# Two chosen experts per query instead of all four: attention on rows of x, VectorE transposes, 32-row value tiles

## The chip, the cores and the metric

The kernel runs on one core of a Trainium2 chip. The metric is the device time of one execution in microseconds (us). The core has five engines that each work through their own list of instructions: PE (TensorE, matmul and weight loads), DVE (VectorE), ACT (ScalarE), POOL (GpSimd) and SP, which issues most DMAs. They meet only at semaphores.

## The reference

There are four batches of S = 1088 positions. Two blocks follow each other.

1. A sketched attention without softmax. For each of four heads of 32 numbers, `phi(x)` is the outer product of two 8-number sketches, `S1 x` and `S2 x`, so 64 features. With `kv = phi(k)^T v` and `z = sum phi(k)`, the result is `phi(q) kv / (phi(q) z + 1e-6)`. The heads side by side give x, 1088 x 128 per batch.
2. A mixture of four attention experts on x:

```
logits = x @ w_gate ; topk = the two largest of the four, per position
w = softmax over the two chosen logits
for each expert e:
    q, k, v = x @ wq[e], x @ wk[e], x @ wv[e]          # 128 -> 64
    a = softmax(causal(q k^T / 8))                     # 1088 x 1088
    out += (w of e, where e was chosen) * (a @ v @ wo[e])
```

All numbers are float32. The reference computes every expert for every query and then masks; a query's two other experts do not reach the result.

## The kernel before, in words

Queries and keys come in tiles of 128 (nine of them, the last with 64 rows). For each batch, `prepare` (line 210) makes what the experts need. `sketch` (253) multiplies k and q by the sketches and forms the features, `kvs` (290) sums them, `turn_features` (305) transposes q's features, and `numer` (316) makes numerator and denominator and divides into `xs`. `turn_x` (338) transposes x to `xT`. Then `project` (354) makes q and k of two experts at a time, 512 columns each, `project_v` (365) makes the values of all four experts and the gate's logits, and `gate` (371) ranks the logits.

The attention goes in units of two query tiles and one pair of experts (`units`, 562). For each query tile and expert of the pair, `scores` (441) runs a matmul with 64 rows (q of the expert times k of the expert, line 452). `take` (432) adds the mask and finds the row's maximum on DVE while it copies the scores from PSUM to SBUF. `soften` (437) takes the exponential on ACT. `turns_of` (504) transposes the weights with TensorE, 128 x 128 at a time through PSUM (512), and `evacuate` (66) copies them back, twice on ACT and once on DVE in turn (69, 71). `values` (578) multiplies with the expert's values, 64 output rows per expert (584, 627). `gates` (529) turns the gate weight over the softmax sum (542), line 589 multiplies it in, and `output` (641) applies wo (658) and stores.

All four experts are computed for all queries; the gate's weight is zero where an expert was not chosen.

The order on PE is written out by hand (line 666 on): for each unit the scores come first, then the values of an earlier unit, then the transposes of the unit before, with the pieces of the next batch's preparation woven in between (`weave`, 550). The order on the other engines is left to a scheduler. PSUM is a pool of eight banks of 512 columns, each handed out as it comes free (`bank`, 73), so scores of several tiles can wait in PSUM at once.

Of the kernel before, what the change touches and what calls it, by code (L numbers as in the profile page):

```python
# [19 lines left out]
def kernel(  # L20
# [15 lines left out]

# [11 lines left out]

    cp = ctx.enter_context(tc.tile_pool(name="const", bufs=1))
    p2 = ctx.enter_context(tc.tile_pool(name="p2", bufs=2))
    p4 = ctx.enter_context(tc.tile_pool(name="p4", bufs=4))
    ps = ctx.enter_context(tc.tile_pool(name="ps", bufs=8, space=bass.MemoryType.PSUM))
# [6 lines left out]

    turn = [0]

    def evacuate(out_, in_):
        turn[0] += 1
        if turn[0] % 3 == 0:
            nc.vector.tensor_copy(out_, in_)  # L69
        else:  # L70
            nc.scalar.copy(out_, in_)  # L71

    def bank(name):
        return ps.tile([128, 512], F32, tag="bank", name=name)
# [9 lines left out]
    kvz = const("kvz", [128, 2, D + 1])  # L84

    def load_rows(dst, src, b):
        return nc.sync.dma_start(out=dst, in_=src[b].rearrange("h (t c) d -> (h t) (c d)", c=C))
# [12 lines left out]
    def load(b):  # L100
        load_rows(kin, k, b)
        load_rows(qin, q, b)
        load_v(b)


# [4 lines left out]
    idle = const("idle", [128, 128])  # L110
    nc.vector.memset(idle, 0.0)
    for x, s in enumerate((S1, S2)):
        eng = (nc.sync, nc.scalar)[x]
        if NS == 1:
            ins = eng.dma_start(out=raw[R * x : R * x + R], in_=s)
        else:
            ins = eng.dma_start(out=raw[R * x : R * x + R].rearrange("p d w -> p (d w)"), in_=s.bitcast(I32))
        if x == 0:
            landing = ins
            with tc.issue_after(landing.ins):  # L120
                load(0)
    wqk = const("wqk", [128, 2, E, HD])
    wvg = const("wvg", [128, E * HD + E])
    wo_sb = const("wo", [128, NG, DM])
    with tc.issue_after(landing.ins):
        for x, w in enumerate((wq, wk)):
            nc.sync.dma_start(out=wqk[:, x], in_=w.rearrange("e p d -> p e d"))
        nc.sync.dma_start(
            out=wvg[:, 0 : E * HD].rearrange("p (e d) -> p e d", e=E), in_=wv.rearrange("e p d -> p e d"))
        nc.sync.dma_start(out=wvg[:, E * HD :], in_=w_gate)  # L130
        nc.sync.dma_start(out=wo_sb, in_=wo.rearrange("(g e) h d -> (e h) g d", g=NG))
    if NS == 2:

# [3 lines left out]
        ex, sg, ma, lw = (const(f"S_{n}", [32, 32], I32) for n in ("ex", "sg", "ma", "lw"))  # L137
        lead, last, ok = (const(f"S_{n}", [32, 32]) for n in ("lead", "last", "ok"))
# [33 lines left out]
    SKW = const("SKW", [128, NS, 2, 2, R])  # L172
    nc.gpsimd.memset(SKW, 0.0)

    nc.vector.transpose(ST.rearrange("p n d -> p (n d)"), S_sum.rearrange("p n d -> p (n d)"))
    for h in range(H):
        last = (nc.vector.tensor_copy, nc.scalar.copy, nc.gpsimd.tensor_copy, nc.vector.tensor_copy)[h](
            SKW[32 * h : 32 * h + 32, :, :, h % 2, :], ST[:, :, 0 : 2 * R].rearrange("d n (x r) -> d n x r", x=2))
    mark = [last.ins]

    nc.gpsimd.memset(kT[:, S:], 0.0)
    nc.gpsimd.memset(qT[:, S:], 0.0)
    nc.gpsimd.memset(vp[:, :, :, D:], 1.0)
    nc.gpsimd.memset(vp[64:, NJ - 1, :, 0:D], 0.0)

# [3 lines left out]


# [11 lines left out]
    vts = [const(f"vt{n}", [128, NJ, E * HD + E]) for n in range(2)]  # L202
    for t in vts:
        nc.gpsimd.memset(t[64:, NJ - 1, E * HD :], 0.0)


    nc.scalar.mul(wqk[:, 0], wqk[:, 0], scale)


    def prepare(b):  # L210
        first = b == 0
        xT = p2.tile([128, S], F32, tag="xT", name=f"xT{b}", bufs=1)
        qk = p2.tile([128, 2 * NG, S], F32, tag="qk", name=f"qkT{b}")
        vt = vts[b % 2]
# [38 lines left out]
        def sketch(nm, xT_, j0, j1):  # L253
# [31 lines left out]
            if first:  # L285
                mark[0] = ins.ins
# [454 lines left out]
```

## Time and profile before

| | us |
|---|---|
| median of 3 runs (lowest, highest) | 372.27 (372.18, 372.96) |
| span of the profiled execution | 362.4 |
| median less span | 9.9 |
| PE busy | 351.5 (97%) |
| weight loads (PEld) busy | 252.2 (70%) |
| DVE busy | 238.7 (66%) |
| ACT busy | 227.7 (63%) |
| POOL busy | 54.1 (15%) |
| share of the chain that ended last: PE | 87% |

The record holds no separate time of the profiled execution beside its span; what lies around the span is read as the difference to the median. Rows of the profile are grouped by source line, engine, operation and tiles: "sc<-qkT" is a matmul that writes the tile sc from qkT. A group shows its busy time, the mean of one instruction in nanoseconds, the idle time of the engine ahead of it, and what ended that. PEld is the load of a matmul's stationary operand, which can overlap a running matmul. The granted PE clock was full (1.000) over the whole span.

### The profile page before, as it was taken

Reading aid. Unit: us, or ns where it says so; the run is one execution under the profiler, and the core shown is the slowest. Engines: PE = TensorE matmul, PEld = TensorE weight load, DVE = VectorE, ACT = ScalarE, POOL = GpSimd, SP = SyncE. Lnnn points to the kernel's source line nnn. Section 1 sums busy time; section 2 is a strip of 40 time slices with the busy share of each in tenths; the row PEclk is TensorE's granted clock in tenths of the full one; section 3 lists DMA queues with packets and bytes.
Section 4 is the critical chain, followed back from the end, with each engine's and each line's share of the span. In section 5 each row is a group of like instructions: output and inputs, shape, how many; then the busy total and the mean of one; then the engine's idle time right before and its main releaser. Section 6 shows DMA issues by size and latency. Waiting matters only on the chain.

```text
span 362.4 us, 10207 instructions
## 1 busy us (share of the span) xinstructions
PE 351.5 (97%) x4138; PEld 252.2 (70%) x4138; DVE 238.7 (66%) x808; ACT 227.7 (63%) x557; POOL 54.1 (15%) x77
## 2 busy tenths in 40 slices
PE   8799989999999999999999999999999999999995
PEld 4666659678676777787675857876776656677774
DVE  6559996676656866657846766567755756765652
ACT  2436757658646786666665756856585666746782
POOL 4001184000000552000000281000000010000010
PEclk9999999999999999999999999999999999999999
DMA  7152422100000000000000000000000000000001
GB/s 208 39 173 59 144 74 96 34 3 16 2 14 1 20 5 2 14 4 4 14 16 0 4 19 4 15 2 2 16 16 2 2 14 6 1 2 16 14 5 29
DMA packets 11374, 10.09 MB, mean 28 GB/s; under 512 B 3648, under 2 KB 10304, under 8 KB 11328
## 3 DMA queue, kind: packets, MB, share of 16 engines
q1 hardware_dynamic: 11168, 9.38, 9.4%
q8 instruction: 32, 0.52, 0.6%
q14 instruction: 14, 0.11, 0.1%
q10 hardware_dynamic: 160, 0.07, 0.1%
HBM read 7.22 MB, written 2.23 MB: 26 GB/s over the span
## 4 chain that ended last, share of the span: by engine, by line
PE 87%; DVE 7%; ACT 3%; issue 1%; DMA 0%; DVEq 0%; ACTq 0%
PE tp L512 18%; PE av L584 17%; PE sc L452 15%; PE qk L356 7%; PE po L658 4%; PE vg L368 4%; PE av L542 3%; PE av L627 3%; PE kv L298 2%; PE num L324 2%; PE sc L493 2%; PE tq L310 2%; ACT a L439 2%; PE sc L470 2%; DVE a L434 1%
## 5 line engine op out<-in xcount | busy, mean ns | idle before, releaser
L439 ACT ACTIVATE a<-a,mx 128x256 f32<-128x256 f32 (+8 forms) x136 | 107.5, 792 | 68.9 <-DVE mx L434 68.9
L434 DVE CUSTOM_DVE_ANT_0 a<-sc,mask 128x512 f32<-128x512 f32 (+3 forms) x136 | 74.2, 592 | 22.5 <-PE sc L452 16.8
L512 PE MATMUL tp<-ident,a 128*128 128x128 f32 (+1 forms) x648 | 85.4, 273 | 0.3 <-ACT aT L71 0.3
L512 PEld LDWEIGHTS tp<-ident,a 128*128 128x128 f32 (+1 forms) x648 | 74.2, 140 | 14.7 <-issue 7.7
L71 ACT COPY aT<-tp 128x512 f32<-128x512 f32 (+3 forms) x121 | 62.5, 547 | 12.6 <-PE tp L512 11.3
L584 PE MATMUL av<-aT,vt 128*64 128x256 f32 (+1 forms) x640 | 67.5, 362 | 0.0
L584 PEld LDWEIGHTS av<-aT,vt 128*64 128x64 f32 x640 | 43.3, 137 | 29.9 <-DVE mx L434 8.1
L452 PE MATMUL sc<-qkT 64*128 64x512 f32 (+3 forms) x320 | 63.4, 531 | 0.0
L536 POOL TENSOR_TENSOR rb<-gw,r 128x256 f32<-128x256 f32 (+1 forms) x36 | 21.1, 590 | 258.1 <-DVE r L533 151.2
L69 DVE COPY aT<-tp 128x512 f32<-128x512 f32 (+3 forms) x59 | 36.9, 628 | 18.9 <-PE tp L512 18.7
L452 PEld LDWEIGHTS sc<-qkT 64*128 64x128 f32 x320 | 27.7, 186 | 25.2 <-issue 15.1
L532 DVE TENSOR_SCALAR r<-z 128x4 f32<-128x4 f32 (+1 forms) x36 | 7.5, 207 | 48.4 <-ACT a L439 46.7
L434 DVE CUSTOM_DVE_ANT_0 a<-sc,mask,mx 128x512 f32<-128x512 f32 (+3 forms) x72 | 38.2, 567 | 0.0
L356 PE MATMUL qk<-xT,wqk 128*128 128x512 f32 x64 | 31.4, 601 | 0.5 <-ACT xT L71 0.5
L439 ACT ACTIVATION_READ_ACCUMULATOR a<-a,mx 128x1 f32 x136 | 25.5, 187 | 0.0
L368 PE MATMUL vg<-wvg,xT 128*128 128x260 f32 (+1 forms) x72 | 20.6, 389 | 0.3 <-ACT xT L71 0.3
L71 ACT COPY qkT<-qk 128x512 f32<-128x512 f32 x20 | 11.7, 583 | 11.8 <-PE qk L356 11.8
L658 PE MATMUL po<-wo,yT 128*128 128x128 f32 (+1 forms) x136 | 18.7, 277 | 0.1
L434 DVE DVE_READ_ACCUMULATOR2_ANT mx<- 128x1 f32 x216 | 17.7, 82 | 0.0
L658 PEld LDWEIGHTS po<-wo,yT 128*128 128x128 f32 (+1 forms) x136 | 16.5, 187 | 0.9 <-issue 0.5
L544 ACT COPY rs<-av 128x256 f32<-128x256 f32 (+1 forms) x36 | 11.9, 352 | 8.3 <-PE av L542 8.0
L589 DVE TENSOR_TENSOR yT<-av,rs 128x256 f32<-128x256 f32 x32 | 12.5, 409 | 5.9 <-ACT rs L544 5.9
(123 smaller groups left out, 355.6 us busy)
## 6 DMA issues: line engine op xcount, KB each, us to landing
kin<-in_k_dram SPq DMA_DIRECT2D x4, 544.0 KB, 3.7
qin<-in_q_dram SPq DMA_DIRECT2D x4, 544.0 KB, 5.9
vin<-in_v_dram SPq DMA_DIRECT2D x16, 128.0 KB, 4.9
out_dram<-ob SPq DMA_DIRECT2D x15, 128.0 KB, 1.8
vtl<-in_v_dram SPq DMA_DIRECT2D x8, 16.0 KB, 2.2
wqk<-in_moe_wq_dram SPq DMA_DIRECT2D x1, 128.0 KB, 5.1
wqk<-in_moe_wk_dram SPq DMA_DIRECT2D x1, 128.0 KB, 3.6
wvg<-in_moe_wv_dram SPq DMA_DIRECT2D x1, 128.0 KB, 4.2
```

Source lines behind the costliest of these rows:

```text
L69: nc.vector.tensor_copy(out_, in_)
L71: nc.scalar.copy(out_, in_)
L356: nc.tensor.matmul(t, wt(a), xT[:, 512 * c : 512 * c + 512], start=True, stop=True)
L368: nc.tensor.matmul(t[0:m, 0 : E * HD + E], xT[:, 128 * j : 128 * j + m], wvg, start=True, stop=True)
L434: nc.vector.tensor_tensor_reduce(out=dst, in0=src, in1=msk, scale=-1.0, scalar=most, op0=ALU.add, op1=ALU.min, accum_out=mx)
L439: nc.scalar.activation(out=a, in_=a, func=ACTF.Exp, bias=mx, scale=-1.0, accum_out=z)
L452: nc.tensor.matmul(sc[e], qk[rows, g, 128 * i : 128 * i + 128], qk[rows, NG + g, keys], start=True, stop=True)
L512: nc.tensor.transpose(tp[0:nk, x : x + 128], ats[e][:, 128 * j : 128 * j + nk], ident)
L536: nc.gpsimd.tensor_tensor(out=rb[:, 0 : w // 128].rearrange("p x (e d) -> p x e d", d=HD), in0=gws[:, :, :, None].to_broadcast(wide), in1= ...
L584: nc.tensor.matmul(av[HD * e : HD * e + HD, lo:256], vt[:, j, c : c + HD], aT[:, e, j, lo:256], start=(j == 0), stop=(j == 2 * p + 1))
L589: nc.vector.tensor_tensor(out=yT[:, g], in0=av[:, 0:256], in1=rs, op=ALU.mult)
L658: nc.tensor.matmul(po[0:nq, DM * x : DM * x + DM], yT[:, g, 128 * x : 128 * x + nq], wo_sb[:, g], start=(g == 0), stop=(g == NG - 1))
```

## The change

Each query now has two rows instead of four: one for each expert that the gate chose. The scores are written with x itself as keys. For an expert, q k^T is x (wq wk^T) x^T, so `expert_matrices` makes the four 128 x 128 products `mcat` once. `chosen` multiplies a tile of x with all four (one matmul of 512 columns), and picks two of the four results per query: ACT copies experts 0 and 3 into the two slots of `u`, and four `copy_predicated` on DVE write experts 1 and 2 over them where `sel` says so. `turn_chosen` transposes `u` to `uT`. A score row is then `uT` times `xT`, 128 deep.

The values are x too: the weights are multiplied with x, and the product goes through wv of the slot's three possible experts (`heads`), where the gate's weight is zero for all but the chosen one. `put` applies wo.

The weights are no longer transposed by TensorE. DVE transposes them in blocks of 32 x 32 (`turns` in `step`, `last_step`), which leaves key k of a block on partition k of one of four groups of 32 partitions, and the query group r = 0 to 3 decides the partition group. So `values` runs matmuls of 32 rows in four partition groups, r = 0 to 3, each into its own PSUM bank (4 to 7), and x must stand four times, once in each partition group: `spread_x` copies it with 16 DMAs per batch.

PSUM is now one tile of eight banks. Scores use banks 0 to 3, always two rows of up to 1024 columns; all other work turns over banks 4 to 7, one bank or an even pair (`bank`). Transposes on TensorE (`turn_blocks`) go in halves of 64 rows.

The order is written out on PE, DVE and ACT. Each batch has six steps, with the query tiles (4, 2), (5, 1), (3), (6, 0), (7) and (8). A step gives the scores, takes and exponentials of its tiles, then the DVE transposes of the step before (`left`), then the work listed in `gaps_of`: values of groups A (tiles 0, 6, 7, 8; done in the next batch's first step), B (4, 5) and C (1, 2, 3), the outputs, and the next batch's preparation. Sketches always run in two accumulated parts; the feature products of later batches stay on POOL. At the start, DVE's transposes of k and half of q now come ahead of the splitting of S1 and S2 into float32 parts.

The diff, cut to its core:

```diff
-    ps = ctx.enter_context(tc.tile_pool(name="ps", bufs=8, space=bass.MemoryType.PSUM))
+    ps = ctx.enter_context(tc.tile_pool(name="ps", bufs=1, space=bass.MemoryType.PSUM))
...
+    P = ps.tile([128, 8, 512], F32, tag="P", name="P")
+    flat = P.rearrange("p k c -> p (k c)")
+    def bank(n=1):
+        k = turn[0] % 4
+        if n == 2 and k % 2:
+            k = (k + 1) % 4
+        turn[0] = k + n
+        return 4 + k
...
+    xrep = const("xrep", [128, NC, DM])
+    GROUPS = {"B": (4, 5), "C": (1, 2, 3), "A": (0, 6, 7, 8)}
+    COL = {"B": 0, "C": 128, "A": 0}
...
+    def spread_x(b):
+        for s in range(4):
+            nj = (NC - s + 3) // 4
+            for r in range(4):
+                nc.sync.dma_start(out=xrep[32 * r : 32 * r + 32, s : s + 4 * (nj - 1) + 1 : 4],
+                                  in_=xs[32 * s : 32 * s + 32, 0:nj])
+    def turn_blocks(ins, dst, copy=None):
+        n, k0 = len(ins), bank(2)
+        for x, a in enumerate(ins):
+            for h in range(2):
+                rows = slice(64 * h, 64 * h + 64)
+                nc.tensor.transpose(P[:, k0 + h, 64 * x : 64 * x + 64], a[rows], ident[rows, rows])
+        (copy or nc.scalar.copy)(dst.rearrange("p n (h q) -> p n h q", h=2),
+                                 P[:, k0 : k0 + 2, 0 : 64 * n].rearrange("p h (n q) -> p n h q", n=n))
...
+    def expert_matrices():
+        wT = p2.tile([128, 2, NG, DM], F32, tag="a", name="wT", bufs=3)
+        for x in range(2):
+            turn_blocks([wqk[:, x, 2 * g : 2 * g + 2, :].rearrange("p e d -> p (e d)") for g in range(NG)], wT[:, x])
+        k0 = bank(2)
+        for g in range(NG):
+            for e in range(2):
+                rows = slice(64 * e, 64 * e + 64)
+                nc.tensor.matmul(P[:, k0 + e, DM * g : DM * g + DM], wT[rows, 0, g], wT[rows, 1, g],
+                                 start=True, stop=True)
+        nc.scalar.mul(mcat.rearrange("p (g e) d -> p e g d", g=NG),
+                      P[:, k0 : k0 + 2, 0 : NG * DM].rearrange("p e (g d) -> p e g d", g=NG), scale)
...
-        def project(a, c):
...
-        def project_v(j):
...
+            nc.tensor.matmul(P[:, k0, E * j : E * j + E], m_.xT[:, 128 * j : 128 * j + 128], wg, start=True, stop=True)
+        V.tensor_tensor(out=pr, in0=ch[:, :, 0::2], in1=ch[:, :, 1::2], op=ALU.mult)
+        V.tensor_copy(sel[:, :, 0:4:3], ch[:, :, 0:4:3])
+        V.tensor_copy(sel[:, :, 2:5:2], pr[:, :, ::-1])
+        V.tensor_tensor(out=sel[:, :, 1:6:4], in0=ch[:, :, 1:3], in1=pr, op=ALU.subtract)
...
+    def chosen(b, i):
+        m_, k0 = batch(b), bank()
+        nc.tensor.matmul(P[:, k0], m_.xT[:, 128 * i : 128 * i + 128], mcat.rearrange("p e d -> p (e d)"),
+                         start=True, stop=True)
+        u = p4.tile([128, 2, DM], F32, tag="u", name=f"u{b}_{i}", bufs=3)
+        c = P[:, k0].rearrange("p (e d) -> p e d", e=E)
...
+        nc.scalar.copy(u[:, 0], c[:, 0])
+        nc.scalar.copy(u[:, 1], c[:, 3])
+        V = nc.vector
+        for x in (1, 2):
+            for s in range(2):
+                V.copy_predicated(u[:, s], m_.sel[:, i, 3 * s + x : 3 * s + x + 1].bitcast(I32).to_broadcast([128, DM]),
+                                  c[:, x])
+        return u
...
-    def scores(b, i, g, qk, z):
...
-    def turns_of(name, i, ats, aT, q0):
...
-    def gates(name, z, gws, w):
...
+    def step(b, tiles):
+        m_, name = batch(b), f"{b}_{tiles[0]}"
+        a = p2.tile([128, 2, 1024], F32, tag="a", name=f"a{name}", bufs=3)
+        mx = p4.tile([128, 2, 2], F32, tag="mx", name=f"mx{name}")
+        at, base = {}, 0
+        for i in tiles:
+            at[i] = base
+            base += 128 * i + 128
+        for s in range(2):
+            for i in tiles:
+                c, end = at[i], at[i] + 128 * i + 128
+                while c < end:
+                    n = min(end, c // 512 * 512 + 512) - c
+                    nc.tensor.matmul(flat[:, 1024 * s + c : 1024 * s + c + n], m_.uT[:, i, s],
+                                     m_.xT[:, c - at[i] : c - at[i] + n], start=True, stop=True)
+                    c += n
+        for s in range(2):
+            for x, i in enumerate(tiles):
+                n = 128 * i + 128
+                cols = slice(at[i], at[i] + n)
+                m = mx[:, s, x : x + 1]
+                take(a[:, s, cols], flat[:, 1024 * s + at[i] : 1024 * s + at[i] + n], mask[:, 1024 - n :], m)
+                soften(a[:, s, cols], m, m_.z[:, i, s : s + 1])
+        def turns():
+            for i in tiles:
+                n, u0 = blocks(i), unit(i)
+                nc.vector.transpose(aT[GRP[i]][:, 0:n, u0 : u0 + 2].rearrange("p c s k -> p s c k"),
+                                    a[:, :, at[i] : at[i] + 32 * n].rearrange("p s (c k) -> p s c k", k=32))
+        return turns
...
+    def last_step(b):
...
+    def values(b, grp):
+        tiles, units = GROUPS[grp], UNITS[grp]
+        last = {(i, r): min(4 * i + r, NC - 1) for i in tiles for r in range(4)}
+        for c in range(blocks(tiles[-1])):
+            for r in range(4):
+                us = [x for x, (i, s) in enumerate(units) if c <= last[i, r]]
+                if us:
+                    assert us[-1] == len(units) - 1
+                    rows = slice(32 * r, 32 * r + 32)
+                    nc.tensor.matmul(P[:, 4 + r, COL[grp] + 32 * us[0] : COL[grp] + 32 * len(units)],
+                                     xrep[rows, c], aT[grp][rows, c, us[0] :],
+                                     start=(c == 0), stop=(c == max(last[i, r] for i in tiles)), skip_group_check=True)
+    def keep(b, c0, k0, n):
+        nc.scalar.copy(batch(b).yT[:, k0 : k0 + n].rearrange("p u r q -> p r u q"),
+                       P[:, 4:8, c0 : c0 + 32 * n].rearrange("p r (u q) -> p r u q", q=32))
...
+    def shares(b, j0, j1, nq=128):
+        m_, js = batch(b), slice(j0, j1)
+        r = p4.tile([128, NJ, 2], F32, tag="r", name=f"r{b}_{j0}")[0:nq, js]
+        nc.gpsimd.tensor_scalar_add(r, m_.z[0:nq, js], 1e-9)
+        nc.vector.reciprocal(r, r)
+        gw = m_.gw[0:nq, js].rearrange("p j (s x) -> p j s x", s=2)
+        nc.gpsimd.tensor_tensor(out=gw, in0=gw, in1=r[:, :, :, None].to_broadcast([nq, j1 - j0, 2, X]), op=ALU.mult)
...
+        def heads(self, i):
+            m_, k0, nq = batch(self.b), bank(), size(i)
+            for s in range(2):
+                u = KEPT[GRP[i]] + unit(i) + (s if i < 8 else 0)
+                quarters = slice(0, 4) if i < 8 else slice(2 * s, 2 * s + 2)
+                nc.tensor.matmul(P[0:nq, k0, 64 * X * s : 64 * X * s + 64 * X],
+                                 m_.yT[:, u, quarters].rearrange("p r q -> p (r q)"),
+                                 wvx[:, X * s : X * s + X].rearrange("p e d -> p (e d)"), start=True, stop=True)
+            hb = self.hb[i] = p4.tile([128, 2 * X, HD], F32, tag="hb", name=f"hb{self.nm}_{i}", bufs=3)
+            nc.vector.tensor_tensor(out=hb[0:nq], in0=P[0:nq, k0, 0 : 2 * X * HD].rearrange("p (x d) -> p x d", d=HD),
+                                    in1=m_.gw[0:nq, i, :, None].to_broadcast([nq, 2 * X, HD]), op=ALU.mult)
+            nc.gpsimd.tensor_tensor(out=hb[0:nq, 1:3], in0=hb[0:nq, 1:3], in1=hb[0:nq, 4:6], op=ALU.add)
...
+    TILES = [(4, 2), (5, 1), (3,), (6, 0), (7,), (8,)]
...
+    def outs(b, *lists):
+        os, f = [Out(b, l) for l in lists], []
+        for n, o in enumerate(os):
+            h = [lambda o=o, i=i: o.heads(i) for i in o.tiles]
+            f += h[:1] + ([os[n - 1].turn] if n else []) + h[1:] + ([os[n - 2].put] if n > 1 else [])
+        return f + [os[-1].turn] + ([os[-2].put] if len(os) > 1 else []) + [os[-1].put]
...
+    def gaps_of(b):
...
+        else:
+            gaps[0] += [lambda: values_a(b - 1), lambda: spread_x(b)] + U(b, 0, 1)
+            gaps[1] += mix(outs(b - 1, (0,), (6, 7), (8,)), U(b, 6, 7))
+            gaps[2] += U(b, 8)
+        gaps[3] += [lambda: values_bc(b)]
+        o = outs(b, (1, 2), (3, 4), (5,))
+        if b + 1 < B:
+            n = b + 1
+            gaps[1] += [lambda: begin_k(n)]
+            gaps[2] += [lambda: sketch(n, "k", 0, 4, G), lambda: sketch(n, "k", 4, NJ, G), lambda: begin_q(n, 0, C),
+                        lambda: kvs(n), lambda: load_next(n + 1) if n + 1 < B else None]
+            gaps[3] = [lambda: sketch(n, "q", 0, 4, G), lambda: sketch(n, "q", 4, NJ, G)] + gaps[3]
+            gaps[4] += [lambda: turn_features(n, 0, 8), lambda: turn_features(n, 8, 13),
+                        lambda: turn_features(n, 13, 18), lambda: numer(n, 0, 5), lambda: numer(n, 5, NJ)] + o[:4]
...
-        for b in range(B):
-            coming, ahead, later = prepare(b + 1) if b + 1 < B else (None, [], [])
...
+    with tc.manual_schedule(engines={mybir.EngineType.PE, mybir.EngineType.DVE, mybir.EngineType.Activation}):
+        first_part()
+        load_next(1)
+        left = None
+        for b in range(B):
+            tiles = TILES if b else [(3,), (4, 2), (5, 1), (6, 0), (7,), (8,)]
+            gaps = gaps_of(b)
+            for n, t in enumerate(tiles):
+                turns = last_step(b) if t == (8,) else step(b, t)
+                if left:
+                    left()
+                left = turns
+                if n == 0 and b:
+                    shares(b - 1, 0, 1)
+                    shares(b - 1, 6, 8)
+                    last_shares(b - 1)
+                if n == 3:
+                    shares(b, 1, 6)
+                for f in gaps[n]:
+                    f()
+        left()
+        b = B - 1
+        shares(b, 0, 1)
+        shares(b, 6, 8)
+        last_shares(b)
+        values_a(b)
+        for f in outs(b, (0,), (6, 7), (8,)):+            f()
```

## The prediction

> **What bounds the kernel now.** I read the engine totals first, then the chain of waits in order of time, then the totals of one stretch of time, and last the groups by form for prices.
>
> The page's totals:
>
> ```profile
> span 362.4 us, 10207 instructions
> PE 351.5 (97%) x4138; PEld 252.2 (70%) x4138; DVE 238.7 (66%) x808; ACT 227.7 (63%) x557; POOL 54.1 (15%) x77
> ```
>
> TensorE is busy 97% of the span. The chain of waits says whether that is dense work; these pieces are from the middle (start, length, what):
>
> ```profile
> 121.66 1.10 PE qps L267 x70
> ...
> 123.02 0.89 PE po L658 x8
> 123.91 1.72 PE qk L356 x4
> ...
> 130.24 1.70 PE sc L452 x8
> ...
> 156.64 1.30 PE num L324 x80
> ...
> 160.60 1.31 PE tp L512 x12
> 161.91 3.42 PE sc L452 x16
> ...
> 214.75 1.70 PE sc L452 x8
> ```
>
> The same piece (sc, x8) stands at 130.24 and at 214.75: one batch takes 84.51 us. The stretch between them:
>
> ```profile
> 130.24:214.75 84.51, 84.51 (x998) 61.54 (x998) 54.66 (x193) 57.05 (x142) 15.04 (x16) 1.00 0.03 8
> ```
>
> Columns: length, then busy time of PE, weight loads, DVE, ACT, POOL, then clock, DMA share and GB/s. PE never stops; DVE and ACT have 30 us to spare. A batch now is TensorE work and nothing else. It remains so only while what PE waits for comes early.
>
> **Prices.** The trace records a float32 matmul twice (32 projections of 512 columns in the program, x64 in the groups), a transpose once.
> - Full-array matmul: qk, four records, 1.72 us: 0.86 us per 512 columns, 1.68 ns per column. po: 0.222 us per 128 columns (0.89/4).
> - sc: x16 are eight matmuls of 64 rows, as four pairs of 512, 384, 512 and 512 columns: 1920 columns in 3.42 us with the tail, 1.78 ns each. Counted singly they would need twice that at qk's rate, so the two 64-row halves run side by side.
> - num: 80 records of 64x64 tiles in 1.30 us, 16 ns each, 65 ns per four: four tiles at once, though 33 columns stream in less. The 64 weight columns set this.
> - tp: 12 full transposes in 1.31 us, 0.109 us each.
>
> Vector and scalar prices, by form:
>
> ```profile
> L434 DVE CUSTOM_DVE_ANT_0 a<-sc,mask 128x512 f32<-128x512 f32 x88 | 57.2, 686 | 15.4 <-PE sc L452 12.8 <-PE sc L493 2.6
> L439 ACT ACTIVATE a<-a,mx 128x1024 f32<-128x1024 f32 x16 | 18.2, 1141 | 2.2 <-DVE mx L434 2.2
> L589 DVE TENSOR_TENSOR yT<-av,rs 128x256 f32<-128x256 f32 x32 | 12.5, 409 | 5.9 <-ACT rs L544 5.9
> L224 DVE STREAM_TRANSPOSE qT<-qin 128x544 f32<-128x544 f32 x8 | 9.3, 1177 | 0.2 <-DMA qin<-in_q_dram 0.2
> L233 DVE STREAM_TRANSPOSE kT<-kin 128x1024 f32<-128x1024 f32 x4 | 5.0, 1238 | 0.0
> L651 DVE COPY ob<-po 128x128 f32<-128x128 f32 x1 | 0.3, 291 | 0.9 <-PE po L647 0.9
> ```
>
> Instructions on DVE overlap by some 0.07 us: in the timeline a 128-column take follows the one before after 0.21 us, a 512-column one after 0.61. So a take costs 0.075 + 1.05 ns per column, a DVE transpose 0.07 + 1.07 ns per column (L233), an exponential the mean of its row (0.29 + 0.83 ns per column).
>
> **What the Trainium skill says.**
> (1) "TensorE: Matmul & The Clock Gate", Architectural detail: PE can pull weight loads ahead, ACT and DVE are strict FIFO. The ledger below rests on it; no row of this trace shows or contradicts it.
> (2) Same page, LDWEIGHTS (loading the stationary operand): a load costs its columns over 1.2 GHz whatever its rows: 107 ns for 128, 53 for 64. The trace is near it: 65 ns per four 64-column loads at once, tail included; I take 0.112 us for 128.
> (3) Same page, Part 3: four 32-row tiles ran at once, 3.07x for 512 columns. The trace shows two row halves at once; no 32-row tile.
> (4) Same page, Part 1: over 3.4 us idle, PE's clock halves. The trace held clock 1.00 in 10 to 20 us with PE busy 7.44 of 10.
>
> **The change, part by part, for one batch.** TensorE:
> - Removed: 162 tp transposes (648 in four batches, 17.7 us), values on 128x64 tiles (about 20: L584 67.5 us in four batches, and L627), qk and vg (31.4 and 20.6 us in four batches), the turns of the gates (L542).
> - Scores (L439, L466 of the changed kernel, as all lines from here): 9216 columns + 1088 at 1.68 ns: 17.3 us. Half the rows of now, but each 128 deep, so nothing runs side by side.
> - chosen (L398): 9 x 0.86 = 7.7. gate (L359): two loads each, 9 x 0.224 = 2.0.
> - values (L487): 74 groups of four 32-row matmuls. Taken as four at once, a group costs the larger of two weight loads (0.224) and its columns (128: 0.213, 160: 0.267, 192: 0.32, 224: 0.373): B 5.4, C 4.35, A 9.25, sum 19.0.
> - heads (L531): 18 x 0.32 = 5.8. put 18 x 0.222 = 4.0. Transposes in 64-row halves (L229): 63 blocks x 0.112 = 7.0. num 2.4, kv 2.1 as now. Sketches: 288 records, four at once, 72 x 0.06 (qps: 70 records in 1.10 us) = 4.2.
> - Sum 71.4 us, against 84.5: 13 us less.
>
> DVE: takes 12, transposes 12, 36 copy_predicated 8, heads 4.2, gate 3.4, numerators 2.4, k and q 3.6, shares 1: 47 us. ACT about 13.5 for exponentials and 17 for copies. Neither is a bound. The copying of x over the four row quarters, 16 DMAs on SP (2.3 MB, 11 us at the 205 GB/s of the first 10 us), starts after values A (15 us) and is read at 57: 30 us of cover. The output DMAs behind it on SP have the same.
>
> copy_predicated has no row: L651 reads the same size from PSUM; four for a tile take 0.9 us with overlap. Bounds: 0.17 each (the shortest DVE rows) to 0.45; all nine tiles lie in waits of PE, so -2 to +8 us per batch.
>
> **The order.** PE, DVE and ACT each run a fixed order: scores of a step; its takes; the transposes of the step before; then the filling. Scores use PSUM banks 0 to 3 alone; everything else turns over banks 4 to 7, a pair for each transpose group, and a bank is rewritten only after its reader is done. I followed each engine through a middle batch with the prices above, 0.16 us for a matmul's tail, 0.05 to 0.1 per hop. Work and wait of PE:
>
> 1. (4,2): work 14.8, wait 5.5. values A needs tile 8's transpose, behind both takes: 2.8. Choosing 0 and 1 waits for ACT's copy of all four banks: 1.2. The turn waits for ACT copies and copy_predicated: 1.7.
> 2. (5,1): 10.8, wait 4.9. The first turn of heads waits for takes, 2.3 us of transposes and two multiplications on DVE, then POOL (0.4): 2.7. Banks held by copy_predicated: 0.6, 1.3, 0.3.
> 3. (3): 7.0, wait 6.7. The turn of tile 8: 3.25 behind takes, transposes (2.3), copy_predicated. kv waits for the key features on POOL (L280, 1.95 + 2.39): 3.5.
> 4. (6,0): 15.3, wait 1.6. values B wants all four banks; ACT empties the sketch only after four exponentials.
> 5. (7): 11.2, wait 3.7. ACT's feature copies stand behind two exponentials: 2.2; then heads, POOL, x: 1.5.
> 6. (8): 12.3, wait 5.6. DVE does a take, 2.25 of transposes and 2.0 of gate before heads: 2.5; then each choice waits for the bank of the one before: 3.1.
>
> Sum 71.4 + 28.0 = 99.4 us a batch, 14.9 more than now. So the removed PE work comes back, twice over, as round trips.
>
> **Whole span.** Front: SKW now comes after kT and half of qT on DVE, 12.0 us to the first sketch against 7.2; then gate, choice, turn: first scores at 33 (now 26). First batch to its end: 125. Two middle batches: 199. Last batch without the next one's preparation and with its tail (values A, keep, heads, turn, put, DMA 1.8): 92. Sum 416 us, against the profiled 362.4. The median 372.27 is 9.9 above that span; I keep 9.9: **426 us**.
>
> **Rivals.**
> A. PE stays fed (the not-slower side). If the orders fit so that waits vanish, the span is 33 + 4 x 71.4 - 12 (first batch's part in the front) + 15 tail = 322, 332 us in all. It decides where a middle batch waits under 13 us instead of 28: the forecast is 54 us over, about 15 for each of some 3.6 batches' worth of steps. For it: no engine is full (PE 72%). Against: each wait above is an order of instructions that the built program shows.
> B. The 32-row tiles run two at a time, not four: values cost 38 us a batch instead of 19, on PE with nothing beside it: 426 + 76 = 502. At 3.07 of 4 it is 449. Against: num has four tiles at once.
> C. DVE's transposes with block-strided output cost L224's 2.16 ns per column instead of L233's 1.07: steps 1, 2, 3, 5, 6 wait some 10 us more per batch: 466.
> D. The waits halve PE's clock (the skill's page above): a window at half clock costs 1.7 us, an estimate from its 3.4; my longest wait is 3.5, so some two per batch: 440.
> E. The change doesn't do what it says: excluded, the program has 17 exponentials a batch where there are 34 (L439 x136).
>
> **How the numbers follow.** Ledger, with D's part and small errors of it (395 to 455): 0.60. B or C, whole or in part (455 to 510): 0.18. In between, waits partly hidden (373 to 395): 0.07. A (below 371.5): 0.13. Within 0.2%, about what a measurement of this kernel can tell from no change: 0.02. That gives faster 0.13, same 0.02, slower 0.85. The range 375 to 490 leaves out A, no change, and the worst of B (0.05). The likeliest's own range is 395 to 455. The unknown prices (copy_predicated -7 to +28 in all) lie within.
>
> **What would show it.** PE busy near 290 of 416 us; waits of PE's weight loads on DVE and ACT where there are none now. L487: four records within about 0.11 us if four tiles run at once, 0.21 if B. L453 near 1.07 ns per column, or 2.2 if C. L408 near 0.23. The chain of waits should name DVE and ACT for a third. It is wrong if PE is above 90% busy in the middle, if a batch repeats in under 88 us, or if a DMA of xrep ends waits.

## The result, and the profile after

The changed kernel takes 478.17 us (median of 4 runs, 472.87 to 481.39), the kernel before 372.23 beside it: 1.302 times as long, 95% interval 1.280 to 1.324. Forecast were 426 us; the direction was right, the loss of 106 us is about twice the 54 forecast. Some runs of a kernel are slower than its others; medians are over all runs (for the changed kernels within 3 us of those of the faster ones), ratios and profiles are of the faster runs alone.

The page's totals of the changed kernel, and two of its rows by slice (the span in 40 slices of 11.9 us; PEclk is the granted TensorE clock in tenths, 9 for 0.9 or more):

```profile
span 476.8 us, 12480 instructions
PE 381.3 (80%) x5480; PEld 280.5 (59%) x5480; DVE 196.1 (41%) x527; ACT 136.7 (29%) x352; POOL 62.7 (13%) x132
...
PE   5978778698876977599788786789797787788795
...
PEclk9555787689889898979789897859978898889899
```

PE is busy 381 us where the forecast expected near 290, and the last row says most of why: in the profiled run before, the clock was 1.000 over the whole span; now its mean is 0.846. Slices 2 to 4, the front, are at half.

The chain of waits, at the first scores, at the same point of three later batches (step (4, 2)), and inside the second batch:

```profile
41.86 3.80 PE P L439 x4
...
149.00 3.47 PE P L439 x12
152.47 0.02 issue
152.49 0.82 DVE a L419
153.32 0.01 DVE mx L419
153.33 0.47 DVE a L419
153.80 0.01 DVE mx L419
153.80 1.22 DVE aTA L473
155.03 0.13 DVE r L511 x2
155.16 0.01 issue
155.17 11.26 PE P L487 x254
...
259.35 3.47 PE P L439 x12
...
371.83 3.47 PE P L439 x12
```

A middle batch repeats after 110.35 and 112.48 us (84.51 before, 99.4 forecast). Ahead of values A (155.17) stands the wait of the forecast's step (4,2): two takes, then tile 8's transpose, 2.70 us from the end of the scores; forecast 2.8. So at this point the order works as it was read. What is new is in the stretches; columns as in the prediction (length, busy time of PE, weight loads, DVE, ACT, POOL, then clock):

```profile
149.00:259.35 110.35, 89.17 (x1366) 66.91 (x1365) 46.33 (x121) 33.17 (x86) 16.90 (x28) 0.89 0.15 37
259.35:371.83 112.48, 92.62 (x1365) 69.58 (x1365) 46.32 (x121) 33.08 (x86) 15.67 (x26) 0.85 0.11 26
...
0.00:41.86 41.86, 30.84 (x492) 22.84 (x492) 16.96 (x56) 9.41 (x24) 5.80 (x25) 0.62 0.42 109
```

I cut each span into slices of half a microsecond and took PE's busy time of each times its clock. That parts a span into three terms: work as it would be at full clock, idle, and what half clock added to the work. Each table of these terms rests on one profiled run per kernel.

| us | span | work at full clock | idle | added by half clock |
|---|---|---|---|---|
| whole | 476.8 | 315.5 | 95.5 | 65.7 |
| to the first scores (41.86) | 41.9 | 18.6 | 11.0 | 12.3 |
| first batch, to 149.00 | 107.1 | 67.8 | 21.3 | 18.1 |
| second batch | 110.4 | 77.6 | 21.2 | 11.6 |
| third batch | 112.5 | 77.0 | 19.9 | 15.6 |
| last batch and tail | 105.0 | 74.6 | 22.2 | 8.2 |

Work and idle make 411.0 us; the forecast's span, at full clock, was 416. The fit hides two errors: work is 315.5 where PE was to be busy near 290, and idle 95.5 where that leaves 126. The third term, 65.7 us, is what it lacked. Whether it is really the cause, or only a way of counting, is what the experiments ask first.

### The profile page after: what moved, and what is told of

Read it like the earlier page. It is cut to its first block, busy times and chain, and to the rows that moved or that the text cites. A ratio compares the mean times of both kernels' runs of the same rounds, so it can differ in the third digit from the quotient of the medians.

```text
span 476.8 us, 12480 instructions
## 1 busy us (share of the span) xinstructions
PE 381.3 (80%) x5480; PEld 280.5 (59%) x5480; DVE 196.1 (41%) x527; ACT 136.7 (29%) x352; POOL 62.7 (13%) x132
## 3 DMA queue, kind: packets, MB, share of 16 engines
q1 hardware_dynamic: 30256, 18.43, 15.6%
## 4 chain that ended last, share of the span: by engine, by line
PE 63%; DVE 18%; ACT 8%; issue 5%; POOL 3%; DMA 2%; SPq 0%; ACTq 0%; POOLq 0%; DVEq 0%
PE P L487 18%; PE P L439 16%; PE P L398 6%; PE P L531 5%; DVE a L419 5%; DVE u L408 5%; PE P L229 4%; PE P L325 3%; PE P L309 3%; PE P L287 3%; PE P L548 3%; ACT a L423 2%; DVE aTA L453 2%; POOL kp L296 2%; PE P L466 2%
## 5 line engine op out<-in xcount | busy, mean ns | idle before, releaser
L419 DVE CUSTOM_DVE_ANT_0 a<-P,mask 128x640 f32<-128x640 f32 (+4 forms) x64 | 46.6, 756 | 116.7 <-PE P L439 116.7
L439 PE MATMUL P<-xT,uT 128*128 128x512 f32 (+3 forms) x192 | 79.3, 567 | 1.4 <-ACT uT L230 1.4
L423 ACT ACTIVATE a<-a,mx 128x512 f32<-128x512 f32 (+8 forms) x68 | 54.0, 795 | 75.3 <-DVE mx L419 75.0
L408 DVE COPY_PREDICATED u<-sel,P 128x128 f32<-128x128 int32 x144 | 31.8, 293 | 68.3 <-ACT u L404 68.3
L439 PEld LDWEIGHTS P<-xT,uT 128*128 128x128 f32 x192 | 38.4, 221 | 32.1 <-issue 26.9
L398 PE MATMUL P<-mcat,xT 128*128 128x512 f32 x72 | 46.3, 749 | 8.1 <-DVE u L408 5.1
L487 PE MATMUL P<-aTA,xrep 32*128 32x160 f32 (+3 forms) x1080 | 44.0, 318 | 8.2 <-DVE r L511 8.2
L487 PEld LDWEIGHTS P<-aTA,xrep 32*128 32x128 f32 x1080 | 43.3, 204 | 10.5 <-ACT a L423 9.9
L531 PE MATMUL P<-wvx,yT 128*128 128x192 f32 (+1 forms) x144 | 39.0, 431 | 2.2 <-ACT yT L492 1.0
L531 PEld LDWEIGHTS P<-wvx,yT 128*128 128x128 f32 (+1 forms) x144 | 31.4, 244 | 5.8 <-issue 3.0
L229 PE MATMUL P<-ident,hb 64*128 64x64 f32 x144 | 11.9, 257 | 17.3 <-POOL hb L537 11.4
L398 PEld LDWEIGHTS P<-mcat,xT 128*128 128x128 f32 x72 | 14.5, 226 | 17.5 <-issue 9.4
```

The costliest lines, as they stand in the source:

```text
L229: nc.tensor.transpose(P[:, k0 + h, 64 * x : 64 * x + 64], a[rows], ident[rows, rows])
L398: nc.tensor.matmul(P[:, k0], m_.xT[:, 128 * i : 128 * i + 128], mcat.rearrange("p e d -> p (e d)"), start=True, stop=True)
L408: V.copy_predicated(u[:, s], m_.sel[:, i, 3 * s + x : 3 * s + x + 1].bitcast(I32).to_broadcast([128, DM]), c[:, x])
L419: nc.vector.tensor_tensor_reduce(out=dst, in0=src, in1=msk, scale=-1.0, scalar=most, op0=ALU.add, op1=ALU.min, accum_out=mx)
L423: nc.scalar.activation(out=a, in_=a, func=ACTF.Exp, bias=mx, scale=-1.0, accum_out=z)
L439: nc.tensor.matmul(flat[:, 1024 * s + c : 1024 * s + c + n], m_.uT[:, i, s], m_.xT[:, c - at[i] : c - at[i] + n], start=True, stop=True)
```

## The experiments

Theory CLOCK: the ledger's sum of work and waits was right, and its waits, with something else, kept PE at half clock for much of the time. Rival WORK: PE's work and waits are larger than the ledger had them, and the clock is a side effect. The kernel after was not run again beside the experiments; the kernel before was, with medians of 370.66 to 371.47 us (372.23 beside the kernel after).

**Filling the waits.** Idle matmuls on PE, in the waits of the trace after; nothing else moves. The first multiply zeros, the others the identity matrix.

```diff
+    def fill(n, k=0):
+        zero = zeros[0]
+        while n > 0:
+            c = min(n, 4)
+            nc.tensor.matmul(P[:, k, 0 : 128 * c].rearrange("p (n c) -> p n c", c=128), zero,
+                             zero[:, None, :].to_broadcast([128, c, 128]), start=True, stop=True)
+            n -= c
...
-            gaps[0] += [lambda: values_a(b - 1), lambda: spread_x(b)] + U(b, 0, 1)
+            gaps[0] += hole(9, 4) + [lambda: values_a(b - 1), lambda: spread_x(b)] + hole(3) + U(b, 0, 1, f=2)
```

`fill(n, k)` writes n x 128 columns into PSUM bank k, and `hole(n, k)` puts it at that place; the other waits got theirs in the same way. Everywhere:

> The waits stay; idle matmuls on PE stand in them (front and all batches), sized just under the waits of the trace after (0.4 to 4.4 us each). Theory CLOCK (the ledger of work and waits was right, PE ran at half clock for about 110 of 477 us): mean clock at least 0.97, time 412 to 430, near the forecast 426. Rival WORK (PE's work and waits are simply larger than the ledger had them): clock may rise, but the time stays at 470 to 490, since idle matmuls only add work.

Measured: 438.83 us (437.93 to 439.64), clock 0.983. In the front and the first batch's first two steps alone:

> Idle matmuls only in the waits of the front and of the first batch's first two steps (to about 80 us). CLOCK: the loss of about 24 us there goes, the rest stays: 450 to 460, clock about 0.90. WORK: 475 to 485.

Measured: 469.83 us (467.82 to 472.81), clock 0.879. From the first batch's third step on:

> Idle matmuls only in the waits from the first batch's third step on. CLOCK: the loss of about 42 us there goes: 430 to 445, clock about 0.92, with half clock left before 80 us. WORK: 475 to 490.

Measured: 448.63 us (447.90 to 450.65), clock 0.942. And six tenths of every fill:

> fill_all with six tenths of its idle matmuls (its fills outlasted the waits by some 16 us in all). If waits under about 1.6 us leave the clock alone, as in the stretches measured by themselves, the clock stays at 0.95 or above and the overshoot shrinks: 425 to 438. If every wait counts: clock about 0.92, time 440 to 455.

Measured: 450.02 us (446.37 to 453.90), clock 0.950.

The totals of fill_all, with the row of its clock:

```profile
PE 394.3 (90%) x5688; PEld 276.5 (63%) x5688; DVE 195.0 (45%) x527; ACT 136.6 (31%) x352; POOL 62.1 (14%) x132
...
PEclk9998999999989999999989999999989999999999
```

More work for PE made the kernel 39 us faster: WORK is out. But all four missed the times that CLOCK, or for fill_less the limit of 1.6 us, had given them. The three terms say by what:

| us | span | work at full clock, fills included | idle | added by half clock |
|---|---|---|---|---|
| after | 476.8 | 315.5 | 95.5 | 65.7 |
| fill_all | 436.1 | 387.7 | 41.8 | 6.6 |
| fill_less | 446.9 | 363.1 | 61.8 | 22.0 |
| fill_front | 466.8 | 333.6 | 80.4 | 52.8 |
| fill_middle | 445.9 | 367.1 | 56.4 | 22.3 |

In fill_all half clock gives back 59 us; idle and fills together are 114.0 (387.7 - 315.5 + 41.8) where idle was 95.5. These 18.5 us are fills that outlast their waits and waits that grow when PE comes to them sooner. With six tenths of the fills it is still 14 (47.6 + 61.8 - 95.5), so the larger part does not look like oversize; how it divides I did not separate. So of the 66 us at least 41 (the spans' difference) are half clock's, since idle matmuls only add work. The rest may be cover that slow matmuls gave to the other engines; that is not shown. fill_front brought its stretch to clock 1.00 up to 70 us (21.9 us of loss before 80 us became 2.6), but lost 50.1 after 80 us where the kernel after lost 43.8, and so gained 8 us instead of some 24: it is 14.3 us ahead when the second batch's scores start, and 10 at the end. fill_less left six waits over 1.6 us where the kernel after has 21, and was to take 425 to 438 us if shorter ones are harmless; it took 450, with 22 us of half clock. A limit for the single wait does not describe it.

**The clock by itself.** The kernel has pieces where PE is busy without a wait and the clock falls nevertheless. The timeline of the kernel after (start, length, what, tile rows*columns, output x columns):

```profile
240.58 2.05 PE L466 MATMUL P<-xT,uT 128*64 128x64 f32 x12
242.57 2.17 PE L359 MATMUL P<-wg,xT 128*128 128x4 f32 x18
244.60 2.33 PE L531 MATMUL P<-wvx,yT 128*128 128x192 f32 x8
```

No wait stands in these, but matmuls of 4 columns (the gate), and from 245.2 to 248.6 the clock is half. So a kernel of nothing but such pieces was run. In a first one, the waits and the tile pieces had been mixed:

> Computes nothing of the reference: bursts of matmuls with waits of known length, to measure the clock by itself. Stretches: bursts of 4 matmuls of 512 columns (3.4 us) with waits of about 0.6, 1.1, 1.8 and 2.9 us; bursts of 12 (10.3 us) with waits of 1.1, 1.8 and 2.9; then 64-row tiles of 33 columns, 32-row tiles of 160 columns, and 128-column matmuls without waits. Theory SHARE (a stretch of a few us with too small a busy share halves the clock, however short its single waits): clock below 1 already at waits of 1.8 us in bursts of 4. Theory of the forecast (only an idle stretch of over 3.4 us does): clock 1.00 in all. Theory SMALL (small tiles alone keep the clock down): below 1 in the tile stretches.

Its record showed tile work running inside the waits, so the waits said nothing; its tiles gave the first hint (64x64 tiles of 33 columns and 32-row tiles both at 0.50). With the order fixed; both kernels work on zeros throughout and ran once:

> Computes nothing of the reference: measures the clock by itself, each stretch followed by 24 full matmuls of 512 columns. First full matmuls with real waits on DVE: bursts of 3.4 us with waits of about 0.9, 1.6, 2.1 and 2.7 us, then bursts of 6.9 and 13.8 us with waits of 2.7. Then without waits: 64 rows alone, 32 rows alone, four 32-row tiles together, four 64x64 tiles of 33 columns, full matmuls of 4 columns, of 128 columns. Theory SHARE (waits and an unused part of the array count alike in a few us): half clock at 2.1 us and more in the short bursts, not in the long ones; half clock at 32 rows alone, at 33 columns and at 4 columns, not at four 32-row tiles nor at 128 columns. Rival (waits alone): clock 1.00 in all stretches without waits.

The stretches with waits, first bursts of 3.4 us with waits of 0.92, 1.58, 2.12 and 2.65 us, then bursts of 6.9 and 13.8 us with 2.65 (columns as above, without ACT: the clock stands after POOL):

```profile
32.26:78.48 46.22, 37.06 (x82) 14.27 (x80) 8.24 (x10) 0.00 (x0) 1.00 0.00 0
98.78:151.91 53.13, 37.30 (x83) 14.43 (x81) 14.91 (x10) 0.00 (x0) 1.00 0.00 0
172.21:239.13 66.92, 45.67 (x83) 17.49 (x81) 20.32 (x10) 0.00 (x0) 0.87 0.00 0
259.43:315.20 55.77, 34.57 (x67) 13.51 (x65) 20.46 (x8) 0.00 (x0) 0.91 0.00 0
338.93:382.13 43.20, 32.60 (x64) 13.33 (x63) 10.23 (x4) 0.00 (x0) 0.88 0.00 0
420.00:478.00 58.00, 47.47 (x109) 20.08 (x107) 10.21 (x4) 0.00 (x0) 1.00 0.00 0
```

Waits of 1.58 us leave the clock alone, those of 2.12 halve it, for about one burst in two. In the timeline of that stretch a burst takes 3.70 us at full clock and up to 1.7 more when it was caught:

```profile
178.33 3.70 PE L50 MATMUL P<-w 128*128 128x512 f32 x8 [2.12 <-DVE sink L82]
184.16 5.35 PE L50 MATMUL P<-w 128*128 128x512 f32 x8 [2.12 <-DVE sink L82]
191.63 3.70 PE L50 MATMUL P<-w 128*128 128x512 f32 x8 [2.12 <-DVE sink L82]
197.46 5.40 PE L50 MATMUL P<-w 128*128 128x512 f32 x8 [2.12 <-DVE sink L82]
```

The stretches without waits, in this order: 64 rows alone; 32 rows alone; four 32-row tiles together; four 64x64 tiles of 33 columns; 4 columns; 128 columns:

```profile
500.33:526.34 26.01, 26.01 (x62) 11.21 (x61) 0.00 (x0) 0.00 (x0) 1.00 0.00 0
560.00:640.00 80.00, 80.00 (x302) 80.00 (x302) 0.00 (x0) 0.00 (x0) 0.50 0.00 0
672.00:698.00 26.00, 26.00 (x776) 26.00 (x772) 0.00 (x0) 0.00 (x0) 1.00 0.01 4
735.00:775.00 40.00, 39.36 (x1423) 38.43 (x1418) 0.00 (x0) 0.00 (x0) 0.50 0.02 5
810.00:866.00 56.00, 56.00 (x274) 56.00 (x274) 0.00 (x0) 0.00 (x0) 0.52 0.00 1
890.00:922.00 32.00, 32.00 (x290) 32.00 (x288) 0.00 (x0) 0.00 (x0) 1.00 0.01 2
```

PE is busy for 98% or more of each of the six windows, and in three of them it has half its clock. So the rival, waits alone, is out. SHARE (what counts is how much of the array works over a few microseconds) came out in part:

- 32 rows alone and 4 columns fell to half clock within 6 us of their start, without a wait, and four 32-row tiles and 128 columns kept the clock, as it said. The 64x64 tiles fell behind 3.41 us with 1.4 us of gaps in their issue, and then stayed at half to their end, for 58 us. That they bring the clock down without gaps is not shown, only that they do not bring it back.
- The long bursts did not come as it said: those of 6.9 us are at 0.88, and of the four waits between the bursts of 13.8 us one halved the clock too, from 477.64 on, at the very end of the line shown.

The record of the clock shows why long bursts do not protect. In every trace of this case the clock changes only at points that lie whole multiples of 3.41 us apart, so time falls into windows of 3.41 us. Three windows in the stretches with waits, each with the one behind it:

```profile
180.68:184.09 3.41, 1.35 (x4) 0.28 (x2) 2.02 (x1) 0.00 (x0) 1.00 0.00 0
184.09:187.51 3.42, 3.35 (x4) 1.51 (x5) 0.01 (x1) 0.00 (x0) 0.50 0.00 0
...
276.25:279.67 3.42, 1.53 (x4) 0.38 (x2) 1.86 (x1) 0.00 (x0) 1.00 0.00 0
279.67:283.08 3.41, 2.65 (x6) 1.25 (x7) 0.70 (x1) 0.00 (x0) 1.00 0.00 0
...
474.23:477.64 3.41, 1.19 (x3) 0.19 (x1) 2.18 (x1) 0.00 (x0) 1.00 0.00 0
477.64:481.05 3.41, 2.98 (x4) 1.43 (x5) 0.38 (x1) 0.00 (x0) 0.50 0.32 94
```

PE is busy 1.35 of 3.41 us in the first (0.40), 1.53 in the second (0.45), 1.19 in the third (0.35). All 12 full-clock windows of these stretches with a busy share of 0.41 or less are followed by half clock, all with 0.45 or more by full clock. So a wait of 2.12 us counts when it falls into one window, and is harmless when enough of it lies in the next one; 1.58 us always leave at least 0.54. The kernel after agrees: of its 22 falls, 16 follow a window with PE busy for 0.40 or less, its waits taken together, and no window that kept the clock is below 0.44. The other six follow windows with a share of 0.44 to 1.00. Small matmuls stand in all six (64x64 transposes, 33 or 4 columns); how much each kind counts was not measured.

The skill's rule that the prediction used ("TensorE: Matmul & The Clock Gate", Part 1: no idle gaps over about 3.4 us) holds as to the length of a stretch, since the half-clock stretches of the second batch are 3.41 us or twice that. As to what starts one, the measurement decides: 2.12 us of wait can be enough here, and so can no wait at all. The same page's section "A second HAM failure mode: psum-queue depth-cycling" (PE idling briefly between groups of matmuls, so that the clock goes to and fro) fits this kernel better; the prediction did not use it.

So the start of the front is explained. PE waits from 7.35 to 11.72 us for the first sketch, and the clock falls at 9.69, behind a window with PE busy 1.07 of 3.41 us:

```profile
6.28:9.69 3.41, 1.07 (x3) 0.19 (x1) 2.64 (x16) 0.61 (x1) 0.00 (x0) 1.00 1.05 187
9.69:13.11 3.42, 1.39 (x50) 1.39 (x53) 1.11 (x6) 2.24 (x4) 0.20 (x1) 0.50 0.89 232
```

Why it stays down until 47.2 is argued only: from 12 to 36 us come key sketches (64x64 tiles, 32 columns), key sums (33 columns), numerators (33) and the gate (4), with waits of 0.5 to 1.7 us between. Such pieces do not always take the clock down. The kernel before ran sketches and key sums at full clock. It had idle matmuls on both sides of its first sketch; the change kept those ahead of it alone, 4.37 us too early:

```profile
12.00:16.00 4.00, 3.29 (x136) 3.25 (x136) 1.88 (x2) 0.43 (x2) 0.00 (x0) 1.00 0.02 5
```

**Are the waits where the ledger put them?** Three edits take waits away, by order and by moving work to another engine; PE's work stays the same. First the DVE transposes, from ahead of a step's filling work to behind it:

```diff
-                if left:
+                if left and n == 3:
                     left()
-                left = turns
+                    left = None
...
                 for f in gaps[n]:
                     f()
-        left()
+                if left:
+                    left()
+                left = turns
+                if n == 5:
+                    left()
+                    left = None
```

> Moves the DVE transposes of the step before from ahead of a step's filling work to behind it, except in step (6, 0), where the values need them at once; tile 8's come at the end of their own step. Theory LEDGER (PE waits where DVE's fixed order puts transposes ahead of what PE needs): per middle batch the wait of values A (2.7) goes, about 1.8 of the 2.5 before the first turn of heads, 1.3 of the 2.9 before the turn of tile 8, up to 1.5 in step (8): 7 us a batch, some 25 in all, and a little clock: 440 to 455. Rival (the waits are round trips that move to another link): 470 to 480.

Measured: 451.69 us (446.74 to 453.14), clock 0.869. Second, the later batches' key features:

```diff
-            gaps[2] += [lambda: sketch(n, "k", 0, 4, G), lambda: sketch(n, "k", 4, NJ, G), lambda: begin_q(n, 0, C),
+            gaps[2] += [lambda: sketch(n, "k", 0, 4, V), lambda: sketch(n, "k", 4, NJ, V), lambda: begin_q(n, 0, C),
```

> The key features of later batches on DVE instead of POOL. LEDGER: the wait of kv for POOL (3.0 us per middle batch, three times) shrinks by about 1.5 to 2.5: 469 to 475. Rival (the copies on ACT ahead of the products are what is late): within 2 us of 478.

Measured: 474.55 us (471.37 to 485.31), clock 0.842. In the profiled runs PE's waits for the key features fell from 8.8 us (on POOL) to 5.2 (on DVE). The runs spread over 14 us, so the gain of 3.6 lies where it was expected but is not secured by the time. Third, both, with the turn of tile 8 put behind the key sketches, and the first two heads ahead of the feature transposes:

```diff
-            gaps[2] += U(b, 8)
+            gaps[2] += [lambda: choose(b, 8)]
...
-            gaps[4] += [lambda: turn_features(n, 0, 8), lambda: turn_features(n, 8, 13),
-                        lambda: turn_features(n, 13, 18), lambda: numer(n, 0, 5), lambda: numer(n, 5, NJ)] + o[:4]
+            gaps[4] += o[:2] + [lambda: turn_features(n, 0, 8), lambda: turn_features(n, 8, 13),
+                        lambda: turn_features(n, 13, 18), lambda: numer(n, 0, 5), lambda: numer(n, 5, NJ)] + o[2:4]
```

> left_late and features_dve together, with the turn of tile 8 behind the key sketches and the first two heads of step (7) ahead of the feature transposes. LEDGER: some 12 of the 21 us of waits per middle batch go, 40 us in all, and with fewer waits fewer half-clock stretches, 10 to 20 us: 415 to 435, clock about 0.90. Rival (waits move on): above 450.

Measured: 432.43 us (431.84 to 447.36), clock 0.893. All three times lie where the ledger expected them, but the split does not: left_late was to take 25 us of waits away and took 10.9 of idle and 14.3 of half clock; order3 was to take 40 of waits and 10 to 20 of half clock, and took 21.7 and 25.7. To that extent the times are luck. The second and third batches of order3, each from the scores of step (4,2) to the next:

```profile
146.80:239.97 93.17, 78.84 (x1367) 58.70 (x1365) 48.39 (x123) 32.63 (x87) 12.59 (x26) 1.00 0.18 44
239.97:335.69 95.72, 82.77 (x1367) 61.86 (x1366) 48.61 (x123) 32.86 (x87) 11.31 (x24) 0.95 0.13 31
```

The second batch's waits sum to 14.3 us, none over 1.6, and its clock is 1.00 without any fill: 93.2 us instead of 110.4. The wait of values A there is 1.55 us, now on the transpose alone. The third batch has waits no longer than these, 13.0 us in all, and still lost 5.1 us to half clock: no single wait decides it.

**The price of choosing.**

```diff
-        for x in (1, 2):
+        for x in ():
             for s in range(2):
...
```

> The changed kernel without its copy_predicated (the four per tile): the slots keep experts 0 and 3, the rest runs as before. It prices the choosing on the path. LEDGER: each tile's 0.9 us of DVE lies in a wait of PE, and waits that name it sum to 25.7 us in the trace after; with a little clock 445 to 460. Rival (ACT's copies or the bank are what is late): above 468.

The kernel leaves out the four `copy_predicated` of each tile. Measured: 443.81 us (439.93 to 447.79), clock 0.887 in the profiled run, just under the range. Idle falls by 15.8 us (95.5 to 79.8), half clock's part by 20.5 (65.7 to 45.2). So the choosing is on the path, with 15.8 us of idle where 25.7 were expected, and the clock more than doubles what it costs. The order runs show about the same proportion.

**Order and fills together.** The edits of order3, and `fill` in the waits that its trace shows, the front's included.

> order3 with idle matmuls in its remaining waits, front included. The profile of order3 has 317 us of PE work (counted at full clock), 74 of idle and 40 lost to half clock. If the three terms stand for themselves (LEDGER plus CLOCK), the 40 go but for some 7, and fills that outlast their waits cost 5 to 10: 397 to 412, clock at least 0.97. Rival (clock and waits don't add up so): above 420. It is not expected to reach the kernel before (371).

Measured: 413.37 us (411.56 to 415.70), clock 0.983, 1.128 times the kernel before (1.111 to 1.146). Work with fills 372.2, idle 30.6, half clock 6.8: idle and fills are 12 us more than order3's idle of 73.9, a little over what I had allowed, so the time is 1.4 us above the range. This is the fastest version of the changed design that was run. It stays slower than the kernel before, and no run points to one that would beat it: the second batch of order3, at clock 1.00 and with no wait over 1.6 us, takes 93.2 us where the kernel before takes 84.5.

## Why the prediction was wrong

By its own steps:

- **Direction: right; bound: right in kind.** The kernel waits on round trips: PE is at 80% (forecast 70%), the chain of waits gives DVE and ACT 26% of the span where a third was named. So rival A, PE fed, is false: a middle batch waits 21 us. None of the forecast's three signs of being wrong came up, as none of them was for the clock; PE busy near 290 us, named as a sign of being right, failed.
- **Order: right in kind, waits put too high.** Per step of the second batch (forecast; measured at full clock):

| step | work | wait | added by half clock |
|---|---|---|---|
| (4,2) | 14.8; 15.9 | 5.5; 4.5 | 1.7 |
| (5,1) | 10.8; 12.3 | 4.9; 4.3 | 1.7 |
| (3) | 7.0; 7.7 | 6.7; 5.9 | 1.6 |
| (6,0) | 15.3; 16.1 | 1.6; 1.0 | 1.6 |
| (7) | 11.2; 11.1 | 3.7; 3.0 | 3.4 |
| (8) | 12.3; 14.5 | 5.6; 2.6 | 1.7 |
| sum | 71.4; 77.6 | 28.0; 21.2 | 11.6 |

  Work was put 6 us too low, waits 7 too high. In part that is one thing counted on the other side: the trace counts a matmul's tail as busy, and two choices cost 1.98 us at full clock where 1.72 were in the ledger. In part prices were low: six output matmuls with tail take 1.74 us (forecast 0.222 each, 1.33), the scores of a batch 18.8 (17.3). That the sum (98.8 against 99.4) fits to 1% is luck to that extent. Step (8), with 2.6 us for 5.6, is the wait furthest off.
- **Rival B, 32-row tiles two at a time: false.** In the clock kernel 100 groups of four tiles of 160 columns take 27.45 us, 0.275 a group; the forecast had 0.267. In the second batch of order3, at clock 1.00, all values take 19.73 us (forecast 19.0).
- **Rival C, slow DVE transposes: false.** copy_predicated is as taken, four in 0.90 us in the chain. The rows of the kernel after, by form:

```profile
L453 DVE STREAM_TRANSPOSE aTA<-a 128x2048 f32<-128x2048 f32 x4 | 9.2, 2306 | 0.0
...
L408 DVE COPY_PREDICATED u<-sel,P 128x128 f32<-128x128 int32 x144 | 31.8, 293 | 68.3 <-ACT u L404 68.3
```

  2306 ns for 2048 columns is 1.13 a column; the difference to the 1024-column form (1241 ns) gives 1.04.
- **The front: half right.** The first sketch comes at 11.72 us (forecast 12.0), the first scores at 41.86 (33). 12.3 us of the front are half clock; in fill_all the first scores stand at 35.33. The ledger called 3.5 us its longest wait, but its own first sketch at 12.0 stood behind a longer one (4.37 measured), which by its own rule costs clock.
- **The time outside the span: wrong.** 9.9 us were kept from the kernel before. The profiled run of the kernel after took 478.73 us at a span of 476.8, so 1.9. The rest of the 9.9 is the clock again: beside the experiments a run of the kernel before took 364.12 us at a span of 362.3 and clock 1.000, another 372.36 at 370.6 and 0.972, and 17 of its 21 runs there are at 0.970 to 0.984. So its usual run loses some clock too; no trace of such a run was kept, and the cause is open.
- **The step that failed: the clock, rival D.** The ledger took 1.00 throughout, and D allowed "some two per batch", 440 us, because only an idle stretch over 3.4 us was thought to count. It named 3.5 us as its longest wait, and did not ask what several shorter ones in one window do. There were seven stretches of 3.4 us in the second batch (23.9 us at half clock), ten in the third (34.1), and in the front one that hardly ended. Its term was put at 14 us and measures 41 to 66. The mechanism stood in the list; its size was read from a rule about single gaps, where PE's busy share in a window of 3.41 us decided most falls (0.41 or less), and small matmuls took part in the others.

On the span, so without the 9.9: forecast 416, measured 476.8, of that 65.7 half clock, and 411.0 left for what the ledger forecast. The measured time lies in the band that the prediction gave to rivals B and C, 455 to 510; neither happened, so that the wide range holds it is luck.

## What to carry to other kernels

A change that takes work from a PE that never waits, and gives it waits and small tiles, loses twice: the waits themselves, and the clock of the work around them. Before trusting a ledger made at full clock, add up the waits in every stretch of a few microseconds, not only the longest one; here about 2 us of 3.4 were enough. Watch matmuls of few columns and single quarter-row tiles too, which went to half clock here without a wait. Shortening waits by order gave back both terms and added no work: order3 is at 432 us with its front still at half clock, fill_all at 439.

## What the hardware showed that was not expected

- The clock changes only on a grid of 3.41 us. With full matmuls, a window with PE busy for 0.41 or less of it (12 of 12) was followed by half clock, one with 0.45 or more by full clock.
- So with bursts of 3.4 us, waits of 1.58 us leave the clock at 1.00; waits of 2.12 us halve it for a part of the bursts (mean 0.87), 1.65 to 1.70 us each time; and of the four waits of 2.65 us between bursts of 13.8 us one did.
- Without any wait, half clock comes from 32 rows alone (0.51 us for 160 columns; an estimate from the forecast's 1.68 ns a column is 0.27 at full clock) and from full matmuls of 4 columns (0.40 us each). Four 64x64 tiles of 33 columns stayed at half for 58 us once they were there. 64 rows alone with 512 columns keep 1.00 (0.87 us each), and so do four 32-row tiles together.
- Small pieces can keep it down: from 12 to 24 us of the changed kernel PE is busy 11.5 of 12 us at clock 0.50.
